# The gated memory mix: how x^T reaches the feed-forward part

## The chip, the cores and the metric

The kernel runs on one core of one Trainium2 chip. The metric is the device time of one execution in microseconds (us). A core has five engines that the text names: TensorE (PE in the profile, with its weight loads as PEld), VectorE (DVE), ScalarE (ACT), GpSimd (POOL) and SyncE (SP), which issues transfers. Each engine works through its own instructions in order and waits on semaphores for the others. Sixteen DMA engines serve the queues of SP, POOL and ACT together.

## What is computed

One input x of 2048 rows by 1024 columns (bf16) goes through two parts, and a gate per row mixes them.

```
g = sigmoid((x * gate_w).sum(-1, keepdims=True))
a = A(x)      # 64 segments of 32 rows, one after the other; 8 memory rows go from each to the next;
              # 32 heads of 128: q, k, v, softmax with a mask, output projection
b = (gelu(x @ w_gate) * (x @ w_up)) @ w_down      # the feed-forward part, inner width 3584
out = g * a + (1 - g) * b
```

## The kernel before

The whole program is one list of operations. `op(engine, make, r=..., w=..., dsem=...)` appends one; the keys in `r` and `w` name what it reads and writes, and the semaphore waits follow from them. The order of the list is the order on each engine: nothing reorders it afterwards. An operation with `dsem` is a DMA, issued by the engine named.

The feed-forward part runs first, in four blocks of 512 rows. A block has a gate/up phase and a down phase. In the gate/up phase 28 steps j (`emit_H`) each make 16 matmuls of 128x512 (L466): eight for the gate, eight for up, with 128 columns of weights as the stationary operand and the block's x^T as the moving one. The results lie in two PSUM banks. A step uses one of two bank pairs, so step j + 2 waits until step j's results are read. ScalarE squares the gate result (L472), VectorE forms the polynomial (L474), ScalarE takes the tanh (L477), and VectorE makes two products (L478 and L481), the second of which writes H and frees the bank. Down (`down_mm`, L511) multiplies H by the down weights in two halves of two row tiles; it uses the other four banks first.

The weights come by SP's queue. `next_slab` (L296) loads slabs of 512 columns, 1 MB each, into four chunks of a large SBUF tile named arena: two slabs after every fourth step, each waiting for TensorE to be done with the chunk that it overwrites. Block 0 also loads the down weights (`load_WD`, L440); blocks 1 and 2 copy weights to a scratch in DRAM for the later part (`copy_wide`, L675). The first two slabs come in halves (L294, L295), the second halves waiting for the last of the first four row tiles and for the first half of slab 0.

The moving operand is x^T: 128 partitions (columns of x within a group of 128), eight groups, 512 rows. x comes as sixteen row tiles t of 128 rows by 1024 columns, `load_rows` (L273): the first four on SP's queue at the very start, the others on POOL's queue into the same four buffers. `emit_xT(t)` makes eight TensorE transposes of 128x128 into a PSUM bank (L346) and one eviction from it into arena, on VectorE (L355), or on ScalarE for tiles 1 and 3 (L353). Between the first four tiles `spin` (L409) makes matmuls of the identity with itself whose result nobody reads: 2, 6, 2 and 8 of them. For tiles 4 to 15 the transposes stand at step j = 12, 16, 20 and 24 of the gate/up phase of the block ahead of the one that needs them.

Two more users of a row tile: `emit_cp(t, half)` copies its transposed rows out of the PSUM bank on ScalarE (L364, L365) in the order that the attention part wants, into xseg, and after the second half POOL issues the transfer of xseg to the scratch xT_scr in DRAM (L369). `emit_gate` multiplies the plain rows by gate_w and sums them on VectorE (L374, L379). The copies stand one and two steps behind the transposes (for the first four tiles: at j = 3t and 3t + 1).

The attention part follows: 64 segments in a written order (PLAN), which stream weights from the scratch through a ring of buffers. It starts after the last down phase.

Of the kernel before, what the change touches and what calls it, by code (L numbers as in the profile page):

```python
# [7 lines left out]
ACTF = mybir.ActivationFunctionType  # L8
# [18 lines left out]
class _Sched:  # L27
# [10 lines left out]
    def op(self, eng, mk, r=(), w=(), dsem=None):  # L38
        o = _Op(eng, mk, dsem)
        deps = []  # L40
        if eng == "pool" and dsem is None:
            w = [*w, ("pool",)]
        for k in r:
            deps += self.w.get(k, ())
            if k[0] == "P":
                deps += [x for x in self.r.get(k, ()) if x.eng != eng]
        for k in w:
            deps += self.w.get(k, ())
            deps += self.r.get(k, ())
        for k in r:  # L50
            self.r.setdefault(k, []).append(o)
        for k in w:
            self.w[k] = [o]
            self.r[k] = []
        seen = set()
        for d in deps:
            if d is o or id(d) in seen:
                continue
            seen.add(id(d))
            if d.eng == eng and d.dsem is None and (eng == "pe" or eng == "sp"):  # L60
                continue
            o.deps.append(d)
            d.sig = True
        self.ops.append(o)
        return o
# [63 lines left out]
def bass_gated_mix__memory_aug_recurrent_mem_tr__geglu_ffn__prompt_kernel(  # L129
# [15 lines left out]
    xf = A_x.flatten_outer_dims()  # L145
# [8 lines left out]
    KC = D // 128  # L154
# [13 lines left out]
    with ExitStack() as es:  # L168
# [23 lines left out]
        def SB(shape, dt, name):  # L192
            return es.enter_context(nc.sbuf_tensor(name, list(shape), dt))
# [20 lines left out]
        ident = SB([128, 128], BF16, "ident")  # L214
# [11 lines left out]
        PBV = [p[:, :].bitcast(BF16) for p in PB]  # L226

        def P(i):
            return ("P", i)

        g = _Sched()
        op = g.op
# [3 lines left out]
        A_X = (4, 5)  # L236
# [8 lines left out]
        def chunk(c):  # L245
            return arena[:, c * (CH // 2):min((c + 1) * (CH // 2), 21 * (CH // 2) + 2048)]

        def A(c):
            return ("A", c)
# [5 lines left out]
           r=[("ident",)], w=[("ident",)])  # L255
        xrow = [chunk(A_M[0])[:, i * 1024:(i + 1) * 1024] for i in range(4)]
        gwb = chunk(A_M[1])[:, 0:1024]
        gpr = chunk(A_M[1])[:, 1024:2048]
        xseg = chunk(A_M[1])[:, 2048:2048 + (GR + 1) * KC * SEG].rearrange("p (s kc c) -> p s kc c", s=GR + 1, kc=KC)
# [7 lines left out]
        misc_rows = A(A_M[0])  # L267
        misc_gate = A(A_M[1])
# [3 lines left out]
        def load_rows(t):  # L272
            op("sp" if t < 4 else "pool", lambda e: e.dma_start(xrow[t % 4], xf[t * 128:(t + 1) * 128, :]),  # L273
               r=[A(A_M[0])], w=[("xrow", t % 4)], dsem=f"xrow{t if t < 4 else t % 4 + 4}")

        for t in range(4):
            load_rows(t)

        def mk_gw(e):
            with nc.allow_non_contiguous_dma(reason="one row to all partitions"):  # L280
# [6 lines left out]
        def load_slab(i):  # L287
            b, jj, k = slabs[i]
            W = B_w_gate if k == "g" else B_w_up
            c = A_W[i % 4]  # L290
            dst = chunk(c).rearrange("p (kc c) -> p kc c", kc=KC)
            src = W[:, jj * 512:(jj + 1) * 512].rearrange("(kc p) c -> p kc c", p=128)
            if i < 2:
                op("sp", lambda e: e.dma_start(dst[:, :, 0:256], src[:, :, 0:256]), r=first[i], w=[("W", i)], dsem=f"rp{4 + i}")  # L294
                return lambda: op("sp", lambda e: e.dma_start(dst[:, :, 256:512], src[:, :, 256:512]), r=[("xrow", 3)] if i == 0 else [("W", 0)], w=[A(c)], dsem=f"a{c}")  # L295
            op("sp", lambda e: e.dma_start(dst, src), r=first[i] if i < 4 else [], w=[A(c)], dsem=f"a{c}")  # L296

        n_slab = [0]
# [1 line left out]
        def next_slab():  # L300
            if n_slab[0] < len(slabs):
                n_slab[0] += 1
                return load_slab(n_slab[0] - 1)

        for rest in [next_slab() for _ in range(2)]:
            rest()
        for _ in range(2):
            next_slab()

# [13 lines left out]
        for side in range(2):  # L323
            op("pool", lambda e, side=side: e.memset(bm[64 * side:64 * side + L, side:side + 1], 1.0),
               r=[("bm",)], w=[("bm",)])
# [10 lines left out]

        def emit_xT(t, eng="dve"):
            b, tt = t // 4, t % 4  # L340
            bank = t % 4 + (0 if b == 2 else 4)

            def mk(e):
                ins = None
                for kc in range(KC):
                    ins = e.transpose(PBV[bank][:, kc * 128:(kc + 1) * 128], xrow[t % 4][:, kc * 128:(kc + 1) * 128],  # L346
                                      ident[:, :])
                return ins
            op("pe", mk, r=[("xrow", t % 4), ("ident",), misc_rows], w=[P(bank)])
            dst = chunk(A_X[b % 2]).rearrange("p (kc r) -> p kc r", kc=KC)[:, :, tt * 128:(tt + 1) * 128]  # L350
            src = PBV[bank].rearrange("p (kc r) -> p kc r", kc=KC)
            if eng == "act":
                op("act", lambda e: e.activation(dst, src, ACTF.Copy), r=[P(bank), A(A_X[b % 2])], w=[("xT", t)])  # L353
            else:
                op("dve", lambda e: e.tensor_copy(dst, src), r=[P(bank), A(A_X[b % 2])], w=[("xT", t)])  # L355

        def emit_cp(t, half):
            bank = t % 4 + (0 if t // 4 == 2 else 4)
            pv = PBV[bank].rearrange("p (kc s c) -> p s kc c", kc=KC, s=4)

            def cp(e):
                ins = None
                for q in (2 * half, 2 * half + 1):
                    ins = e.activation(xseg[:, q, :, 0:NR], pv[:, q, :, EXT:SEG], ACTF.Copy)  # L364
                    ins = e.activation(xseg[:, GR, :, q * EXT:(q + 1) * EXT], pv[:, q, :, 0:EXT], ACTF.Copy)  # L365
                return ins
            op("act", cp, r=[P(bank), misc_gate, ("xseg0",)], w=[("xseg", half)])
            if half:
                op("pool", lambda e: e.dma_start(xT_scr[t, :, :], xseg.rearrange("p s kc c -> p (s kc c)")),  # L369
                   r=[("xseg", 0), ("xseg", 1), misc_gate], w=[("xTscr", t)], dsem="xseg")  # L370
# [34 lines left out]
        def spin(n):  # L405
            def mk(e):
                ins = None
                for _ in range(n):
                    ins = e.matmul(PB[3][:, 0:128], lhsT=ident[:, :], rhs=ident[:, :], start=True, stop=True)  # L409
                return ins  # L410
            op("pe", mk, r=[("ident",)], w=[P(3)])

        for t in range(4):
            emit_xT(t, ("dve", "act")[t % 2])
            spin((2, 6, 2, 8)[t])

        def emit_m0():
            def mk(e):
# [285 lines left out]
        for b in range(4):  # L704
            mine, other = (b % 2) * 4, 4 - (b % 2) * 4
            for j in range(NJ):
# [3 lines left out]
                if b == 0 and j < 12 and j % 3 < 2:  # L710
                    emit_cp(j // 3, j % 3)
# [7 lines left out]
                if b < 3 and j >= 12:  # L719
                    t = (b + 1) * 4 + (j - 12) // 4  # L720
                    if j % 4 == 0:
                        emit_xT(t)
                    elif j % 4 == 1:
                        emit_cp(t, 0)
                    elif j % 4 == 2:
                        emit_gate(t, 0)
                        emit_cp(t, 1)
                    else:
                        emit_gate(t, 1)
# [241 lines left out]
        for s in range(NSEG):  # L971
# [393 lines left out]
            if s == 0:  # L1365
                emit_P("q", 0, (0,))
                def zero(e):
# [4 lines left out]
                   w=[P(B_S), ("gp",)])  # L1372
# [10 lines left out]
                   w=[("bo", x) for x in range(4)])  # L1383
# [178 lines left out]
```

## Time and profile before

| | us |
|---|---|
| runs shown (three): median | 2209.19 |
| lowest and highest | 2204.6 and 2210.04 |
| the profiled execution | 2207.77 |
| its span, first to last instruction | 2205.9 |
| TensorE busy in it | 2104.6 |

Times in the profile count from the first instruction of the span. A row of the timeline begins with its start and its length in us, then the engine, the line of the kernel, the operation, and what it writes and reads; square brackets name how long the engine stood idle before it and who released it. SPq is SP issuing a transfer: the length is that of issuing, not of moving. A row of the DMA view ends with the size of one transfer and the median time from issue to landing of those issued in the stretch asked for. A row of busy time by stretch has, behind the stretch and its length, the busy time of PE, PEld, DVE, ACT and POOL with the number of instructions, the granted TensorE clock, the mean busy share of the sixteen DMA engines, and GB/s. A row of the DMA queues has packets, MB and their share of the sixteen engines' time. The granted TensorE clock of this execution is 0.994 of full speed in the mean.

### The profile page before, as it was taken

Reading aid. Unit: us, or ns where it says so; the run is one execution under the profiler, and the core shown is the slowest. Engines: PE = TensorE matmul, PEld = TensorE weight load, DVE = VectorE, ACT = ScalarE, POOL = GpSimd, SP = SyncE. Lnnn points to the kernel's source line nnn. Section 1 sums busy time; section 2 is a strip of 40 time slices with the busy share of each in tenths; the row PEclk is TensorE's granted clock in tenths of the full one; section 3 lists DMA queues with packets and bytes.
Section 4 is the critical chain, followed back from the end, with each engine's and each line's share of the span. In section 5 each row is a group of like instructions: output and inputs, shape, how many; then the busy total and the mean of one; then the engine's idle time right before and its main releaser. Section 6 shows DMA issues by size and latency. Waiting matters only on the chain.

```text
span 2205.9 us, 78545 instructions
## 1 busy us (share of the span) xinstructions
PE 2104.6 (95%) x35368; PEld 1107.8 (50%) x35424; DVE 1154.8 (52%) x2680; ACT 935.6 (42%) x1960; POOL 461.6 (21%) x814
## 2 busy tenths in 40 slices
PE   9999999999998999999999999999999999999987
PEld 4444444444454555555454545555455555555544
DVE  5716536345054555555555555555555555555554
ACT  4403324133044444544454445444444444444443
POOL 1020020140122222222122222222122222222221
PEclk9999999999999999999999999999999999999999
DMA  8726625346888999999999999999999999999997
GB/s 271 276 70 220 215 58 194 122 148 202 302 302 301 325 326 328 326 338 328 330 317 327 325 319 329 323 324 320 315 323 328 332 330 329 337 333 323 324 325 245
DMA packets 247377, 629.21 MB, mean 285 GB/s; under 512 B 37393, under 2 KB 106081, under 8 KB 246273
## 3 DMA queue, kind: packets, MB, share of 16 engines
q1 hardware_dynamic: 215732, 573.14, 74.5%
q0 software_dynamic: 30112, 50.48, 7.4%
q8 instruction: 278, 4.55, 0.8%
q10 hardware_dynamic: 1196, 0.56, 0.1%
q14 instruction: 59, 0.48, 0.1%
HBM read 596.71 MB, written 34.59 MB: 286 GB/s over the span
## 4 chain that ended last, share of the span: by engine, by line
PE 77%; DMA 15%; DVE 4%; ACT 2%; issue 2%; POOL 0%; SPq 0%; DVEq 0%; POOLq 0%; ACTq 0%
PE pba L1087 13%; PE pbb L1087 12%; DMA ring<-w_scr 11%; PE pbc L897 6%; PE pbb L1279 4%; DMA hT<-xT_scr 3%; PE pba L1279 3%; PE pbc L1258 3%; PE pba L466 2%; PE pbh L466 2%; PE pbg L466 2%; PE pbf L466 2%; PE pbe L466 2%; PE pbb L466 2%; PE pbd L466 2%; PE pbc L466 2%
## 5 line engine op out<-in xcount | busy, mean ns | idle before, releaser
L1087 PE MATMUL pba<-arena,hT 128*32 128x512 bf16 x4416 | 357.1, 383 | 5.1 <-DVE bo L1358 4.4
L1087 PE MATMUL pbb<-arena,hT 128*32 128x512 bf16 x4416 | 355.6, 383 | 1.3 <-issue 1.3
L897 PE MATMUL pbc<-arena,xe 128*32 128x512 bf16 x2208 | 190.0, 381 | 3.4 <-ACT rowsx L996 2.0
L803 POOL DMA_DIRECT2D vt<-v_scr x252 | 140.7, 561 | 146.8 <-PE pba L1087 94.3
L1087 PEld LDWEIGHTS pba<-arena,hT 128*32 128x32 bf16 x4416 | 109.2, 97 | 112.1 <-ACT rows L1074 11.0
L1087 PEld LDWEIGHTS pbb<-arena,hT 128*32 128x32 bf16 x4416 | 113.4, 97 | 99.2 <-DVE hT L1355 6.2
L1087 PE MATMUL pba<-ring,hT 128*32 128x512 bf16 x1286 | 127.2, 384 | 18.5 <-DMA ring<-w_scr 16.7
L1184 ACT ACTIVATE pbd<-pbd 104x320 f32<-104x320 f32 x128 | 53.0, 414 | 215.3 <-DVE pbd L1182 215.3
L1087 PE MATMUL pbb<-ring,hT 128*32 128x512 bf16 x1280 | 126.4, 384 | 7.8 <-DMA ring<-w_scr 7.2
L920 ACT ACTIVATE rows<-pba 128x512 bf16<-128x512 f32 (+1 forms) x130 | 67.1, 516 | 150.2 <-PE pba L1087 126.0
L1194 DVE TENSOR_TENSOR pn<-pbd,rr 104x512 bf16<-104x512 f32 (+1 forms) x256 | 125.7, 491 | 9.3 <-DVE rr L1189 0.6
L920 ACT ACTIVATE rows<-pbb 128x512 bf16<-128x512 f32 x127 | 66.0, 520 | 149.5 <-PE pbb L1087 119.5
L1026 POOL DMA_DIRECT2D qk_scr<-rowsx x60 | 47.5, 792 | 365.2 <-DVE pbd L1178 171.5
L1178 DVE SCALAR_TENSOR_TENSOR pbd<-pbd,mask 104x320 f32<-104x320 f32 x128 | 63.5, 496 | 102.0 <-PE pbd L1171 102.0
L1279 PE MATMUL pbb<-arena,oT 128*32 128x256 bf16 (+1 forms) x2304 | 115.8, 268 | 0.0
L1279 PE MATMUL pba<-arena,oT 128*32 128x256 bf16 (+1 forms) x2320 | 112.7, 269 | 0.1
L477 ACT ACTIVATE arena<-arena 128x512 f32<-128x512 f32 x112 | 70.5, 629 | 97.6 <-DVE arena L474 97.6
L821 POOL DMA_DIRECT2D bo<-b_scr x63 | 35.6, 565 | 341.8 <-PE pba L1087 235.9
L920 ACT ACTIVATE oT<-pbe 128x256 bf16<-128x256 f32 x192 | 73.6, 384 | 48.7 <-PE pbe L1231 47.4
L920 ACT ACTIVATE qk<-pbe 128x512 bf16<-128x512 bf16 x127 | 75.5, 594 | 36.4 <-PE pbe L1133 35.1
L1187 DVE TENSOR_REDUCE mx<-pbd 104x8 f32<-104x320 f32 x128 | 62.9, 491 | 53.5 <-ACT pbd L1184 53.5
L1133 PEld LDWEIGHTS pbe<-ident,rows 128*32 128x32 bf16 (+1 forms) x1560 | 46.0, 96 | 77.6 <-ACT rows L920 50.4
(308 smaller groups left out, 4519.5 us busy)
## 6 DMA issues: line engine op xcount, KB each, us to landing
ring<-w_scr SPq DMA_DIRECT2D x896, 512.0 KB, 5.5
arena<-in_B_w_gate_dram SPq DMA_DIRECT2D x27, 1024.0 KB, 5.4
arena<-in_B_w_up_dram SPq DMA_DIRECT2D x27, 1024.0 KB, 8.3
pn<-qk_scr POOLq DMA_DIRECT2D x63, 128.0 KB, 5.3
qk_scr<-rowsx POOLq DMA_DIRECT2D x60, 128.0 KB, 5.0
arena<-in_B_w_down_dram SPq DMA_DIRECT2D x7, 1024.0 KB, 11.4
arena<-in_A_Wk_dram SPq DMA_DIRECT2D x6, 1024.0 KB, 6.9
arena<-in_A_Wv_dram SPq DMA_DIRECT2D x6, 1024.0 KB, 10.1
```

Of the source, the lines that this page charges most:

```text
L466: ins = e.matmul(PB[bank][:, :], lhsT=wv[:, kc, col:col + 128], rhs=xb[:, kc, :], start=(kc == 0), stop=(kc == KC - 1))
L477: op("act", lambda e: e.activation(tp[q], tp[q], ACTF.Tanh, scale=C_GELU), r=[("tp", q)] + mr, w=[("tp", q)])
L803: op("pool", lambda e, side=side: e.dma_start(vt[p0 + side * EXT:p0 + (side + 1) * EXT, :, :], v_scr[s // GR, h, side::2, s % GR, :, :].re ...
L897: ins = e.matmul(PB[B_X][32 * gq:32 * gq + 32, :], lhsT=xe[:, us[-1], :], rhs=us[gq // 2][0][gq % 2], start=(n == 0), stop=(n == KC - 1), ...
L920: op("act", lambda e: e.activation(dst, src, ACTF.Copy), r=r, w=w)
L1087: ins = e.matmul(PB[bank][32 * gq:32 * gq + 32, :], lhsT=hT[:, kc, :], rhs=us[gq // 2][0][gq % 2], start=(x == 0), stop=(x == KC - 1), ski ...
L1178: op("dve", lambda e: e.scalar_tensor_tensor(out=sv, in0=sv, scalar=scale, in1=mask[0:104, None, :].to_broadcast([104, 8, L]), op0=ALU.mul ...
L1184: op("act", lambda e: e.activation(sv, sv, ACTF.Exp), w=[P(B_S)])
L1187: op("dve", lambda e: e.tensor_reduce(mxv, sv, AX.X, ALU.add), r=[P(B_S)], w=[("mx",)])
L1194: op("dve", lambda e, c0=c0, k0=k0, n=n: e.tensor_tensor(out=pn[0:104, :, c0:c0 + 2 * n].rearrange("p i (two c) -> p i two c", two=2), in0 ...
L1258: ins = e.matmul(PB[B_X][b:b + 32, :], lhsT=oe[:, o * 8 + k, :], rhs=u[c], start=(n == 0), stop=(n == H - 2), skip_group_check=True)
L1279: ins = e.matmul(PB[B_O][32 * q:32 * q + 32, c0:c1], lhsT=oT[:, o % 2, k, :], rhs=u[q // 2][:, (q % 2) * 256 + c0:(q % 2) * 256 + c1], sta ...
```

## The change

The sixteen tiles of x^T are no longer made on TensorE. Each is one transposing DMA from x in DRAM straight into arena, on SP's queue. The first four stand at the head of that queue, where the four plain row loads stood; the plain loads, still needed for the gate, follow behind the four half slabs. The others stay at the same place in the list (j = 12, 16, 20, 24), now as SP operations, and name no chunk that they would have to wait for. The second half of slab 0 waits for the transposed tile 3 where it waited for the plain one. The copies into xseg read arena, where they read PSUM, and so wait for the transposing DMA to land. The spins become one run of 48, behind which the first gate/up matmul stands.

```diff
+        def emit_xT(t):
+            dst = chunk(A_X[t // 4 % 2]).rearrange("p (kc r) -> p kc r", kc=KC)[:, :, t % 4 * 128:(t % 4 + 1) * 128]
+            op("sp", lambda e: e.dma_start_transpose(dst, xf[t * 128:(t + 1) * 128, :]),
+               w=[("xT", t)] + ([("xT", t - 8)] if t >= 8 else []), dsem="xt%d" % (t % 4))
+
         for t in range(4):
-            load_rows(t)
+            emit_xT(t)
...
-                return lambda: op("sp", lambda e: e.dma_start(dst[:, :, 256:512], src[:, :, 256:512]), r=[("xrow", 3)] if i == 0 else [("W", 0)], w=[A(c)], dsem=f"a{c}")
+                return lambda: op("sp", lambda e: e.dma_start(dst[:, :, 256:512], src[:, :, 256:512]), r=[("xT", 3)] if i == 0 else [("W", 0)], w=[A(c)], dsem=f"a{c}")
...
         for rest in [next_slab() for _ in range(2)]:
             rest()
+        for t in range(4):
+            load_rows(t)
         for _ in range(2):
             next_slab()
...
-        def emit_xT(t, eng="dve"):
-            b, tt = t // 4, t % 4
-            bank = t % 4 + (0 if b == 2 else 4)
...
-            op("pe", mk, r=[("xrow", t % 4), ("ident",), misc_rows], w=[P(bank)])
...
-                op("dve", lambda e: e.tensor_copy(dst, src), r=[P(bank), A(A_X[b % 2])], w=[("xT", t)])
-
         def emit_cp(t, half):
-            bank = t % 4 + (0 if t // 4 == 2 else 4)
-            pv = PBV[bank].rearrange("p (kc s c) -> p s kc c", kc=KC, s=4)
+            pv = chunk(A_X[t // 4 % 2]).rearrange("p (kc t s c) -> p t s kc c", kc=KC, t=4, s=4)[:, t % 4]
...
-            op("act", cp, r=[P(bank), misc_gate, ("xseg0",)], w=[("xseg", half)])
+            op("act", cp, r=[("xT", t), A(A_X[t // 4 % 2]), misc_gate, ("xseg0",)], w=[("xseg", half)])
...
-        for t in range(4):
-            emit_xT(t, ("dve", "act")[t % 2])
-            spin((2, 6, 2, 8)[t])
+        spin(48)
```

More of the change, by code (lines that the diff above doesn't have):

```diff
@@ L334, in bass_gated_mix__memory_aug_recurrent_mem_tr__geglu_ffn__prompt_kernel @@
         op("pool", lambda e: e.dma_start(m0, mem0[:, :]), r=[A(A_W[3])], w=[("oe", x) for x in range(NO)], dsem="m0")
-        def emit_xT(t, eng="dve"):
-            b, tt = t // 4, t % 4
-            bank = t % 4 + (0 if b == 2 else 4)
[L343 to L348, printed above, removed]
-            op("pe", mk, r=[("xrow", t % 4), ("ident",), misc_rows], w=[P(bank)])
[L350 to L354, printed above, removed]
-                op("dve", lambda e: e.tensor_copy(dst, src), r=[P(bank), A(A_X[b % 2])], w=[("xT", t)])
         def emit_cp(t, half):
-            bank = t % 4 + (0 if t // 4 == 2 else 4)
-            pv = PBV[bank].rearrange("p (kc s c) -> p s kc c", kc=KC, s=4)
+            pv = chunk(A_X[t // 4 % 2]).rearrange("p (kc t s c) -> p t s kc c", kc=KC, t=4, s=4)[:, t % 4]
             def cp(e):
```

## The prediction

> **What bounds the kernel now.** Page first, for the share of each engine and the chain of work that ended last.
>
> ```profile
> PE 2104.6 (95%) x35368; PEld 1107.8 (50%) x35424; DVE 1154.8 (52%) x2680; ACT 935.6 (42%) x1960; POOL 461.6 (21%) x814
> ...
> PE 77%; DMA 15%; DVE 4%; ACT 2%; issue 2%; POOL 0%; SPq 0%; DVEq 0%; POOLq 0%; ACTq 0%
> ```
>
> TensorE bounds the whole. The change touches the feed-forward part alone, so the second view is busy time by stretch: the first block's gate/up phase, its down phase, and block 1.
>
> ```profile
> 9.80:106.60 96.80, 95.99 (x467) 44.44 (x476) 68.22 (x100) 43.53 (x120) 9.93 (x18) 1.00 0.84 283
> 109.00:157.50 48.50, 48.24 (x222) 21.95 (x225) 4.25 (x7) 2.03 (x4) 6.35 (x12) 1.00 0.24 77
> 157.50:300.00 142.50, 141.81 (x673) 65.56 (x685) 69.88 (x102) 42.43 (x93) 15.62 (x28) 1.00 0.53 176
> ```
>
> TensorE (first number after the length) has no slack: whatever leaves its queue is gained, whatever makes it wait is lost. The DMA share (second last) is 0.84 in the first gate/up phase and 0.53 in block 1 as a whole: the new transfers go where DMA is busiest. The third view is the chain in order of time, here its start and one later transpose group.
>
> ```profile
> 3.70 1.03 PE pbe L346 x8
> ...
> 8.40 1.03 ACT arena L353
> ...
> 9.78 1.67 PE pba L466 x7
> ...
> 55.30 0.45 PE pbe L346 x8
> ```
>
> The first gate/up matmul (L466) starts at 9.78, after four transpose groups and the last eviction. A later group of eight transposes takes 0.45 us on the chain.
>
> **What is removed.** Four groups ahead of 9.78 (counted in the start below) and twelve later ones, 12 x 0.45 = 5.4 us of TensorE time; one of them stands where VectorE is late in block 0, so I count 5.3. Fourteen evictions leave VectorE and two leave ScalarE; save the last of the start (8.40), all lie beside TensorE: nothing. The copies to xseg (L364, L365) read SBUF now; ScalarE's 128x512 takes 0.63 us from SBUF (L477, the group below) and 0.60 from PSUM (L472, in a row further down), so a copy changes by some hundredths either way: nothing, under TensorE's cover.
>
> ```profile
> L477 ACT ACTIVATE arena<-arena 128x512 f32<-128x512 f32 x112 | 70.5, 629 | 97.6 <-DVE arena L474 97.6
> ```
>
> **What one transposing DMA costs (call it T, us of the sixteen DMA engines for 256 KB).** No row shows one. The nearest rows are queue 1 in two stretches with runs of 512 bytes (8 to 12 us) and longer ones (12 to 20 us).
>
> ```profile
> q1 hardware_dynamic: 2226, 1.12, 109.8%
> ...
> q1 hardware_dynamic: 2424, 2.27, 89.4%
> ```
>
> 64 us of engine time for 2226 packets of 503 bytes is 28.7 ns each; 0.894 x 128 us for 2424 of 936 bytes is 47.2 ns. That is 7.2 ns plus 0.043 ns a byte. A plain tile at 47.2 ns for 936 bytes would be 262144/936/16 x 47.2 ns = 0.8 us: the lower end. A transposed tile writes each source row across partitions; if it goes in 32-byte pieces, 8192/16 x 8.6 ns = 4.4 us: the upper end. I take the geometric middle, 1.9 us, because 256-byte reads alone (64 x 18.1 ns) already give 1.2 and the scattered write comes on top. The Trainium skill, "DMA: Bandwidth & Descriptors", Latency and other measured facts, gives a DMA transpose 261 GB/s with a non-contiguous middle dimension, an estimate of 1.0 us a tile; by that the sum below would be about zero. No run here shows it yet.
>
> **The start.** SP's queue and its waits:
>
> ```profile
> 0.75 1.84 SPq L273 DMA_DIRECT2D arena<-in_A_x_dram  x4
> ...
> 6.64 0.37 SPq L295 DMA_DIRECT2D arena<-in_B_w_gate_dram  x1
> 8.34 0.37 SPq L295 DMA_DIRECT2D arena<-in_B_w_up_dram  x1
> ```
> ```profile
> SPq L295 <- DMA arena<-in_A_x_dram: 2.6, 1, 2.6
> ...
> SPq L295 <- DMA arena<-in_B_w_gate_dram: 1.3, 1, 1.3
> ```
>
> SP sits on the last x tile until 6.64 and on the first half of slab 0 until 8.34; those are their landings. The four transposes take the place of the plain loads at the head of the queue, so both landings move by 4(T - 0.8). The matmul then waits for slab 0 instead of for an eviction: at T = 1.9 it starts at 8.34 + 4.4 + 0.2 = 12.9, which is 3.2 later than 9.78. Queued behind on SP are the slab halves and now the four plain x loads (1 MB, some 3 us), ahead of slabs 2 and 3, first needed four steps of 3.46 us (96.8 us over 28) after the start; the gate's VectorE work needs the rows later still: nothing. The clock:
>
> ```profile
> 8.16 0.85 PE L409 MATMUL pbd<-ident 128*128 128x128 bf16 x8
> ```
>
> The spins at the start cost 106 ns each against 56 later (0.45/8), a half-rate array from 3.70 to about 9. The 48 spins need 5.1 us at that rate and begin at the earliest when identity is built, so TensorE is idle for some us before 12.9. If the rate falls back, the same 5.3 us at half rate is 2.7 lost; bounds 0 and 2.7, I take 1.3. The Trainium skill, "TensorE: Matmul & The Clock Gate", Part 1, puts the fall at about 3.4 us of idling; nothing of before shows it. Start: +4.5.
>
> **The later twelve.** They stand in SP's queue behind weight transfers, and ScalarE, in order, now waits for their landing at L364, where it waited for TensorE. Behind that wait stand the next Square (L472), VectorE's three steps (L474, L478, L481), and TensorE, which needs L481 to free its banks two steps later. For t = 4 the transfer ahead is issued at 51.82 and lands 11.3 later (the DMA view of 51.80 to 51.87):
>
> ```profile
> 51.82 1.87 SPq L440 DMA_DIRECT2D arena<-in_B_w_down_dram  x2
> ```
> ```profile
> arena<-in_B_w_down_dram SPq DMA_DIRECT2D x1, 1024.0 KB, 11.3
> ```
> ```profile
> 60.67 0.31 ACT L364 ACTIVATE arena<-pbe 128x192 bf16<-128x192 bf16 x1
> ...
> 64.54 0.69 DVE L481 SCALAR_TENSOR_TENSOR arena<-arena,pba 128x512 bf16<-128x512 f32 x1
> ...
> 65.94 1.89 PE L466 MATMUL pba<-arena 128*128 128x512 bf16 x8
> ```
>
> It lands at 63.1 + T; ScalarE would copy at 60.67. Hidden is only 65.94 - 65.23 = 0.7. Stall: 63.1 - 60.67 - 0.7 + T = 1.7 + T. For t = 5 the queue is still full from t = 4, but TensorE has moved by that first stall: I put it at T - 1.4. The largest of block 1 is t = 10, behind a scratch copy (issued 228.03, landing 9.9 later):
>
> ```profile
> 228.03 0.73 SPq L675 DMA_DIRECT2D w_scr<-in_A_Wv_dram  x1
> ...
> w_scr<-in_A_Wv_dram SPq DMA_DIRECT2D x1, 512.0 KB, 9.9
> ...
> 235.13 0.31 ACT L364 ACTIVATE arena<-pbc 128x192 bf16<-128x192 bf16 x1
> ...
> 236.70 0.60 ACT L472 ACTIVATE arena<-pbe 128x512 f32<-128x512 f32 x1 [0.80 <-PE pbe L466]
> ...
> 239.50 0.69 DVE L481 SCALAR_TENSOR_TENSOR arena<-arena,pbe 128x512 bf16<-128x512 f32 x1
> ...
> 241.68 0.59 PE L466 MATMUL pbe<-arena 128*128 128x512 bf16 x2
> ```
>
> 237.9 - 235.13 = 2.8 late, less ScalarE's idle 0.8 and 241.68 - 240.19 = 1.5 of slack: 0.5 + T. t = 8 (issue 199.51, +8.4, copy 206.61) gives T - 1.0 and t = 9 (213.77, +9.2, copy 220.87) T - 0.2 in the same way:
>
> ```profile
> 199.51 0.59 SPq L675 DMA_DIRECT2D w_scr<-in_A_Wk_dram  x1
> ...
> 213.77 1.31 SPq L675 DMA_DIRECT2D w_scr<-in_A_Wv_dram  x2
> ...
> 206.61 0.31 ACT L364 ACTIVATE arena<-pba 128x192 bf16<-128x192 bf16 x1
> ...
> 220.87 0.31 ACT L364 ACTIVATE arena<-pbb 128x192 bf16<-128x192 bf16 x1
> ```
> ```profile
> w_scr<-in_A_Wk_dram SPq DMA_DIRECT2D x1, 512.0 KB, 8.4
> ...
> w_scr<-in_A_Wv_dram SPq DMA_DIRECT2D x1, 512.0 KB, 9.2
> ```
>
> Block 2's tiles stand right behind a slab with nothing between. For t = 13 that slab is issued at 360.18 and lands 8.1 later, against a copy at 367.70:
>
> ```profile
> 360.18 0.37 SPq L296 DMA_DIRECT2D arena<-in_B_w_up_dram  x1
> ...
> arena<-in_B_w_up_dram SPq DMA_DIRECT2D x1, 1024.0 KB, 8.1
> ...
> 367.70 0.31 ACT L364 ACTIVATE arena<-pbf 128x192 bf16<-128x192 bf16 x1
> ```
>
> 0.6 late, 2.3 hidden as at t = 10: T - 1.7. I price t = 6, 12 and 14, likewise behind a slab, with it. The last tile of each block (7, 11, 15) costs nothing: after its copy come two gate/up steps whose banks are free, then 24 us of down-projection on the other four banks; without that cover it would cost like its neighbours. At T = 1.9: 3.6 + 0.5 + 0.9 + 1.7 + 2.4 + 4 x 0.2 = 9.9. The same late copies delay the xT_scr writes on POOL's queue and the x loads behind them; these are read at the recurrence hundreds of us later: nothing. The recurrence itself is unchanged.
>
> **Sum.** 4.5 - 5.3 + 9.9 = +9.1. The profiled execution took 2207.77 us (span 2205.9), 1.4 under the median 2209.19; 2207.77 + 9.1 = 2216.9, against the median **2218**, +0.4%. At T = 0.8: start -1.2 (slab 0 at 8.34), -5.3, stalls 2.5 + 0.6 + 1.3 = 4.4: -2.1. At T = 4.4: +13.2 + 2.7 - 5.3 + (6.1 + 3.0 + 3.4 + 4.2 + 4.9 + 10.8) = +43.
>
> **Rivals.** (1) The transposed tile is as cheap as a plain one: T below about 1.1, where the sum crosses zero. For it speaks that both read 256 KB of DRAM on sixteen engines; against it the short pieces. Time 2207; with every wait hidden as well, -6.5, 2202.7. (2) The scattered write dominates, T of 3 to 4.4: +25 to +43, 2234 to 2252. For it speaks the fixed 7.2 ns a packet. (3) The tile's eight 128-wide blocks go one after the other, each a small transfer:
>
> ```profile
> b_scr<-ring POOLq DMA_DIRECT2D x2, 16.0 KB, 1.9
> ```
>
> at 1.9 us to land (0 to 120 us), T = 15: start +56, nine stalls some 130, about 2390. Against it: the sixteen-engine queue shows no such serial transfer. The Trainium skill, "VectorE: DVE Perf Modes", The three transpose paths, lists 1309 ns for a 128x128 DMA transpose against 390 on TensorE, a rule against this change; eight of those are an estimate of 10.5 us a tile, some 2330.
>
> **Chances.** Forecast (T 1.4 to 3, 2212 to 2234) 0.47; rival 1 0.30; rival 2 0.15; rival 3 0.08. Under 0.3% (6.6 us) a measurement tells no difference, and T = 1.7 is where the sum passes it: faster 0.05 (the far end of rival 1), same 0.35 (the rest of it and the forecast's low end), slower 0.60. Range 2204 to 2255, which leaves out rival 3 and the ends of 1 and 2.
>
> **What would show it.** On the page L346 and L355 are gone. SP's first wait on x should end at 6.64 + 4.4 = 11, the first L466 start near 13, its first matmuls perhaps at half rate. ScalarE's L364 should wait on a DMA into arena, longest at t = 4 and t = 10, and TensorE on L481 two steps later by 2 to 4 us. A DMA row of the transposes gives T at once: 1.0 at the head of the queue makes rival 1, 10 rival 3. The forecast is wrong if a tile does not keep its place in the queue, so that waits vanish or grow without T, or if TensorE's banks have more slack than these rows give.

## The result, and the profile after

The changed kernel takes 2219.66 us in the median of 20 runs (2208.09 to 2231.89), the kernel before 2206.95 in 20 runs beside it (2201.54 to 2210.98). The ratio is 1.006, 95% interval 1.0046 to 1.0074: 12.7 us slower, where 9 were forecast.

The profiled execution of the changed kernel happens to be the fastest of its twenty. So its stages are read, not its total. Engine shares and chain on its page:

```profile
PE 2101.1 (95%) x35326; PEld 1099.8 (50%) x35326; DVE 1145.3 (52%) x2666; ACT 935.3 (42%) x1958; POOL 460.9 (21%) x814
...
PE 71%; DMA 16%; DVE 7%; ACT 3%; issue 2%; SPq 0%; POOL 0%; DVEq 0%; ACTq 0%
```

Against before, VectorE's share of the chain is 7% where it was 4%: TensorE now waits for VectorE's steps. Busy time by stretch, first of the kernel before (first gate/up phase, the rest of the feed-forward part, the attention part), then of the changed one:

```profile
0.00:108.90 108.90, 103.61 (x528) 50.72 (x539) 71.87 (x105) 47.64 (x124) 13.25 (x39) 1.00 0.82 274
108.90:596.00 487.10, 484.68 (x2260) 222.76 (x2304) 203.72 (x298) 123.08 (x249) 59.32 (x110) 1.00 0.51 167
596.00:2205.90 1609.90, 1516.28 (x32584) 834.31 (x32582) 879.21 (x2278) 764.84 (x1588) 388.98 (x666) 0.99 0.93 322
```
```profile
0.00:119.40 119.40, 106.11 (x503) 48.63 (x504) 64.62 (x94) 44.38 (x114) 12.96 (x38) 0.96 0.90 267
119.40:608.90 489.50, 485.23 (x2242) 218.38 (x2240) 201.10 (x295) 126.47 (x258) 59.48 (x110) 1.00 0.55 170
608.90:2206.30 1597.40, 1509.75 (x32584) 832.76 (x32582) 879.54 (x2278) 764.44 (x1588) 388.44 (x666) 1.00 0.93 324
```

The feed-forward part ends 12.9 us later (608.9 against 596.0), 10.5 of it in the first gate/up phase. The attention part, which the change does not touch, is 12.5 us shorter in this one execution; in the fourteen profiles of this case it takes between 1596 and 1610 us, so that difference is scatter. The 12.9 us agree with the 12.7 between the medians.

Where it goes is read from the starts of the steps in TensorE's timeline, the gate matmuls of step j of a block, before and after:

| block, step | before | after | later by |
|---|---|---|---|
| 0, 0 | 9.78 | 11.20 | 1.42 |
| 0, 1 | 13.02 | 16.69 | 3.67 |
| 0, 6 | 30.29 | 36.71 | 6.42 |
| 0, 8 | 37.19 | 44.08 | 6.89 |
| 0, 15 | 62.49 | 69.27 | 6.78 |
| 0, 16 | 65.94 | 76.12 | 10.18 |
| 0, 17 | 69.84 | 81.26 | 11.42 |
| 1, 0 | 157.46 | 168.00 | 10.54 |
| 2, 0 | 304.28 | 315.88 | 11.60 |
| 3, 0 | 451.11 | 463.97 | 12.86 |

Three things add up: the start (3.7), a jump at steps 6 to 8 (3.2), and after that 6.0 net, in which some 5.2 us of saved transposes are already counted, so 11 us of stalls. (The row of before at 9.78 has seven of the eight matmuls; if the one that is not recorded is the first, step 0 is 1.6 later and not 1.4.) The rows of TensorE's timeline at the start, the jump and the two longest later stalls:

```profile
11.20 3.59 PE L452 MATMUL pba<-arena 128*128 128x512 bf16 x8 [5.13 <-DMA arena<-in_B_w_gate_dram]
...
36.71 1.90 PE L452 MATMUL pba<-arena 128*128 128x512 bf16 x8 [2.59 <-DVE arena L467]
...
76.12 2.96 PE L452 MATMUL pba<-arena 128*128 128x512 bf16 x8 [3.23 <-DVE arena L467]
...
401.52 1.89 PE L452 MATMUL pba<-arena 128*128 128x512 bf16 x8 [2.19 <-DVE arena L467]
```

L452 is the old L466, L467 VectorE's last step of H (old L481), L352 the copy to xseg (old L364). SP's queue, which in the rows of before had the plain loads at its head:

```profile
0.75 5.41 SPq L278 DMA_TRANSPOSE arena<-in_A_x_dram  x4
6.21 0.58 SPq L299 DMA_DIRECT2D arena<-in_B_w_gate_dram  x1
...
8.62 0.81 SPq L300 DMA_DIRECT2D arena<-in_B_w_gate_dram  x1
11.17 0.37 SPq L300 DMA_DIRECT2D arena<-in_B_w_up_dram  x1
...
59.41 7.70 SPq L278 DMA_TRANSPOSE arena<-in_A_x_dram  x1
```

Issuing four transposes takes SP 5.41 us (four plain loads took 1.84), and one issued into a full queue 7.70. So the first half of slab 0 is issued at 6.21, where it was at 2.63, and is down at 11.17, where it was at 8.34. ScalarE's waits in the gate/up phases, summed, and the two at the jump and at tile 4:

```profile
ACT arena L352 <- DMA arena<-in_A_x_dram: 29.2, 12, 4.9
...
ACT arena L352 <- DMA xT_scr<-arena: 5.3, 2, 4.9
```
```profile
32.37 0.36 ACT L352 ACTIVATE arena<-arena 128x192 bf16<-128x192 bf16 x1 [4.86 <-DMA xT_scr<-arena]
...
71.69 0.36 ACT L352 ACTIVATE arena<-arena 128x192 bf16<-128x192 bf16 x1 [4.58 <-DMA arena<-in_A_x_dram]
```

All twelve later tiles are late for ScalarE. The wait at 32.37 is another one: the buffer xseg is not free, since its write to xT_scr has not landed. That wait was not forecast.

### The profile page after: what moved, and what is told of

The parts are those of the page before. It is cut to its first block, busy times and chain, and to the rows that moved or that the text cites. A ratio compares the mean times of both kernels' runs of the same rounds, so it can differ in the third digit from the quotient of the medians.

```text
span 2206.3 us, 78419 instructions
## 1 busy us (share of the span) xinstructions
PE 2101.1 (95%) x35326; PEld 1099.8 (50%) x35326; DVE 1145.3 (52%) x2666; ACT 935.3 (42%) x1958; POOL 460.9 (21%) x814
## 4 chain that ended last, share of the span: by engine, by line
PE 71%; DMA 16%; DVE 7%; ACT 3%; issue 2%; SPq 0%; POOL 0%; DVEq 0%; ACTq 0%
PE pba L1073 12%; PE pbb L1073 12%; DMA ring<-w_scr 11%; PE pbc L883 6%; PE pbb L1265 4%; PE pba L1265 3%; PE pbc L1244 3%; DMA arena<-in_A_x_dram 2%; PE pbe L1190 2%; PE pbe L1119 2%; PE pbd L1157 2%; PE pbe L1217 2%; DMA hT<-xT_scr 2%; PE pbe L452 2%; PE pbh L452 2%; PE pbg L452 2%
## 5 line engine op out<-in xcount | busy, mean ns | idle before, releaser
L1073 PE MATMUL pba<-ring,hT 128*32 128x512 bf16 x1286 | 128.4, 383 | 12.7 <-DMA ring<-w_scr 11.8
```

The lines of the kernel that those rows point to most:

```text
L1073: ins = e.matmul(PB[bank][32 * gq:32 * gq + 32, :], lhsT=hT[:, kc, :], rhs=us[gq // 2][0][gq % 2], start=(x == 0), stop=(x == KC - 1), ski ...
```

## The experiments

"Later by" means the start of the last step of block 3 against the kernel before, in the profiles; it tells a few us apart where the whole time scatters by more. Ratios are whole times against the kernel before on the same chip. bare_price, pool_free and spin_long were run once, so only their profiles are read.

### One part alone: the start, and the later tiles

start_only gives tiles 4 to 15 back to TensorE, with eviction and copies as before (code shortened here and below).

```diff
-        def emit_xT(t):
+        def emit_xT(t, eng="dve"):
+            if t >= 4:
+                return emit_xT_pe(t, eng)
```

> Only tiles 0 to 3 come by transposing DMAs; tiles 4 to 15 are transposed on TensorE and evicted as before. Theory (the loss is the sum of two separate parts, a late start and late copies): the down part of block 3 begins about 6.9 us later than in the kernel before, 3.7 of it at the first gate/up steps and some 3 at step 6, where ScalarE waits for xT_scr; no later wait at the copies; time about 2214. Rival (the start is made up for later, and the twelve later tiles cost everything): under 1 us later, 2207.

later_only does the reverse: `if t < 4`, with the loads and spins of the start as before.

> Only tiles 4 to 15 come by transposing DMAs; the first four and the start are as before. Theory: the first gate/up matmul is back at 9.8 us, ScalarE waits some 29 us in total at the copies for the transposed tiles, and the feed-forward part ends about 6 us later than before; time about 2213. Rival (the start costs everything): 5 us earlier than before, 2202.

start_only: later by 7.9 us, ratio 1.0043 (1.0019 to 1.0067). later_only: 4.5 us, ratio 1.0027 (1.0002 to 1.0053). Together 12.4, against 12.9 for the whole change: the two parts add up, and the start weighs more than the later tiles. That they agree so closely is in part chance, since the jump at steps 6 and 7 is 5.4 us in start_only's profile and 3.2 in the changed kernel's. In start_only the loss is complete at step 7 (8.6 us); nothing after it stalls. In later_only the first matmul is back at 9.65 us, and ScalarE's waits for tiles are as in the whole change:

```profile
ACT arena L374 <- DMA arena<-in_A_x_dram: 28.7, 11, 5.8
```

### Is it the transposing, or the place in the queue?

plain_rows puts a plain DMA of the same bytes, in the same 256-byte pieces, where each transposing DMA stands; arena then holds x untransposed.

```diff
-            op("sp", lambda e: e.dma_start_transpose(dst, xf[t * 128:(t + 1) * 128, :]),
+            op("sp", lambda e: e.dma_start(dst, xf[t * 128:(t + 1) * 128, :].rearrange("r (kc c) -> r kc c", kc=KC)),
```

> Every transposing DMA becomes a plain one of the same 256 KB to the same place, at the same point of SP's queue; so arena holds x untransposed and the products are of other numbers. Theory (the place behind the weights makes two thirds of the lateness, the transfer itself one third): ScalarE's waits for the tiles shrink from 29 us to 15 to 18, the start is 1 to 4 us earlier, and the feed-forward part ends 2 to 5 us later than before. Rival (the transposing itself, its slow transfer and the 4 to 8 us that SP is busy issuing one, makes nearly all): waits under 5 us, and the part ends 5 us earlier than before, 2202.

Neither held. The waits for tiles are not smaller at all, ratio 1.0066 (1.0045 to 1.0088):

```profile
ACT arena L352 <- DMA arena<-in_A_x_dram: 28.9, 11, 5.5
...
ACT arena L352 <- DMA xT_scr<-arena: 9.3, 2, 8.2
```

A plain tile at the same place is as late as a transposed one, though SP issues it in 0.6 to 1.6 us and not in 3.7 to 7.7. So for the later tiles the place behind the weights makes the lateness, and neither the transposing nor SP's long issue does. The start is quicker (step 1 later by 1.8, not 3.7), and there SP's issuing has a part in it: the first slab goes out 1.8 us sooner than in the changed kernel, and the first matmul starts 1.3 sooner.

```profile
0.75 3.67 SPq L278 DMA_DIRECT2D arena<-in_A_x_dram  x4
4.45 0.88 SPq L299 DMA_DIRECT2D arena<-in_B_w_gate_dram  x1
```

The jump at steps 6 and 7, 8.7 us here, is larger than in the changed kernel and hides that; it is taken up below.

bare_price measures a tile by itself: the kernel before, with eight transposing DMAs added in block 0's down phase and eight plain ones in block 1's, all into a chunk that nobody reads at that time.

```diff
+            if b < 2:
+                for i in range(8):
+                    dst = chunk(A_X[b]).rearrange("p (kc r) -> p kc r", kc=KC)[:, :, i % 4 * 128:(i % 4 + 1) * 128]
+                    # b == 0: dma_start_transpose(dst, x tile i); b == 1: dma_start of the same bytes; both wait for the last H
```

> The kernel before with two things added where DMA is nearly idle and nothing waits for them: in block 0's down phase eight transposing DMAs of 256 KB, in block 1's eight plain DMAs of the same bytes to the same places, each in two runs of four. Theory from the plain-rows run (a transposed tile costs hardly more of the DMA engines than a plain one): four back to back take 4 to 6 us transposed and 3.5 to 5 plain. Rival (my estimate of 1.9 us a tile against 0.8): 7.6 us and more against 3.2.

The DMA view of a stretch in which only the transposed tiles move, and of one with only the plain ones:

```profile
DMA packets 4576, 1.14 MB, mean 190 GB/s; under 512 B 4576, under 2 KB 4576, under 8 KB 4576
```
```profile
DMA packets 4280, 1.08 MB, mean 216 GB/s; under 512 B 4280, under 2 KB 4280, under 8 KB 4280
```

That is 262144 bytes in 1.38 us transposed and 1.21 us plain, or 5.5 and 4.9 for four: the theory of this run. But the two are not limited by the same thing. SP issues the transposing DMAs 1.35 us apart (at 123.47, 124.82, 126.17 and 127.52) without waiting for anything, and the DMA engines' busy share, here in tenths over 40 slices of each stretch, falls between them; in the plain stretch they are busy throughout:

```profile
DMA  0999678799999433799999523799999945897999
```
```profile
DMA  9999999999999999999999999999999999999999
```

So 1.38 us is SP's pace, and an upper bound on what a transposed tile costs the DMA engines. From 120.0 to 121.1 us, with issued tiles still queued, they moved at 286 GB/s, from which I estimate 0.92 us a tile. That the transposing itself costs the DMA engines anything is not shown; a plain tile in 256-byte pieces costs more than my 0.8 us.

### Earlier tiles, later copies

If the place is the cause, there are two cures: issue the tiles earlier, or read them later. early_four issues tiles 4 to 15 at steps 8, 12, 16 and 20.

```diff
+                if b < 3 and 12 - 4 <= j < 28 - 4 and (j + 4) % 4 == 0:
+                    emit_xT((b + 1) * 4 + (j + 4 - 12) // 4)
                 if b < 3 and j >= 12:
                     t = (b + 1) * 4 + (j - 12) // 4
-                    if j % 4 == 0:
-                        emit_xT(t)
-                    elif j % 4 == 1:
+                    if j % 4 == 1:
```

> Tiles 4 to 15 are issued four steps (some 14 us) earlier in SP's queue, at steps 8, 12, 16 and 20; the copies stay where they are. Theory (late copies): ScalarE's waits for the tiles fall from 29 us to under 5, TensorE's waits on L467 after step 12 vanish, and the feed-forward part ends 1 to 3 us later than before instead of 12.9; time about 2209. Rival (SP, busy issuing a transpose, holds up the slabs behind it): the same waits move to TensorE waiting for slabs, and the time stays at 2219.

Not one wait of ScalarE for a tile is left, and from step 8 to the end the kernel gains 5.4 us (from 11.7 late to 6.3), as much as the saved transposes. Late copies were the later tiles' whole loss. The total is higher than expected (ratio 1.0043, 1.0017 to 1.0068) because the jump at steps 6 and 7 is 8.6 us in this profile.

later_early joins the early tiles with the start of the kernel before.

> The start as in the kernel before (tiles 0 to 3 on TensorE), tiles 4 to 15 by transposing DMAs issued four steps earlier than in the changed kernel. Theory (with the place in the queue mended only the gain is left): the feed-forward part ends 5 to 6 us earlier than before, 12 times 0.45 us; time about 0.25% under the kernel before. Rival (a transposing DMA costs something wherever it stands): no earlier than before.

Later by -0.2 us, not -5 to -6; ratio 0.9996 (0.9978 to 1.0014). From block 1 on it gains all of its 0.45 us a tile, but block 0 loses 5.2 us up to step 13, 1.6 of it in the jump at steps 6 to 8 and 3.6 at steps 12 and 13. Busy time by stretch, 45 to 65 us, of this kernel and of the kernel before:

```profile
45.00:65.00 20.00, 17.09 (x71) 7.13 (x71) 13.66 (x20) 6.99 (x19) 2.69 (x5) 0.91 1.16 297
```
```profile
45.00:65.00 20.00, 19.59 (x96) 9.03 (x97) 15.17 (x24) 9.91 (x29) 2.69 (x5) 1.00 0.89 315
```

The DMA share is 1.16 (the view counts overlapping packets) against 0.89, although fewer bytes move (297 GB/s against 315), and ScalarE waits 3.7 us for xT_scr at 50.96: what the tile no longer loses, the write behind it does. That the fuller queues make this wait is argued from these rows and tested only by the next kernel. eight_early leaves tiles 4 to 7 on TensorE, too (`if t < 8`, the others early).

> Tiles 0 to 7 on TensorE as in the kernel before; only tiles 8 to 15 (issued in blocks 1 and 2) by transposing DMAs, four steps earlier than in the changed kernel. Theory (block 0 has no DMA time to spare, blocks 1 and 2 have): the feed-forward part ends 3.6 us earlier than before, 8 times 0.45 us; ratio about 0.9984. Rival (the DMAs cost something in any block): less than 1.5 us earlier.

Earlier by 4.5 us, ratio 0.9986 (0.9963 to 1.0009): the gain is in the trace, and the whole time cannot tell it from none. Of the 4.5, 0.96 is there at the end of block 0, where this kernel is the kernel before; so much do two profiles of the same instructions differ, and the change's own gain is the 3.6 of eight groups.

copies_late moves the reader: start as before, tiles 4 to 15 at the place of the changed kernel, copies four steps later.

```diff
                     elif j % 4 == 1:
-                        emit_cp(t, 0)
+                        if j > 16:
+                            emit_cp(t - 1, 0)
...
+                emit_cp(b * 4 + 7, 0)          # ahead of the down phase
+                emit_cp(b * 4 + 7, 1)
```

> The start as in the kernel before, tiles 4 to 15 by transposing DMAs at the place of the changed kernel, and the copies to xseg four steps later (those of a block's last tile ahead of its down phase). Theory (only ScalarE's in-order wait for the tile costs; the DMA's place does not): no wait for a tile, and the feed-forward part ends 4 to 5.4 us earlier than before. Rival (the extra transfers in block 0 hold up other transfers by themselves): a loss of 2 us or more stays in block 0 and the part ends less than 3 us earlier.

Ratio 0.997 (0.9949 to 0.9991): faster than both kernels. In its profile no wait for a tile is left and the part ends 1.9 us earlier; it would be 6.1 but for a jump of 4.1 us at steps 6 and 7, which this execution has although its start is that of before.

### The jump at step 6: POOL's queue

The first write to xT_scr stands on POOL behind the loads of gate_w and mem0, which wait for slabs 2 and 3. pool_free lets both wait for slab 0.

```diff
-        op("pool", mk_gw, r=[A(A_M[1]), A(A_W[2])], w=[("gwb",)], dsem="gwb")
+        op("pool", mk_gw, r=[A(A_M[1]), A(A_W[0])], w=[("gwb",)], dsem="gwb")
-        op("pool", lambda e: e.dma_start(m0, mem0[:, :]), r=[A(A_W[3])], w=[("oe", x) for x in range(NO)], dsem="m0")
+        op("pool", lambda e: e.dma_start(m0, mem0[:, :]), r=[A(A_W[0])], w=[("oe", x) for x in range(NO)], dsem="m0")
```

> As the changed kernel, but on POOL's queue the loads of gate_w and mem0 wait for slab 0 instead of slabs 2 and 3, so that the first xT_scr write behind them is issued earlier. Theory (POOL's queue, held by slabs that land later now, makes the stall at step 6): ScalarE's wait for xT_scr falls from 5.3 us to under 1.5, the jump at step 6 is gone, and the feed-forward part ends 9 to 10.5 us later than before instead of 12.9. Rival (the transfers at the start are slow in themselves): the jump stays.

The jump is gone (step 8 later by 3.5, not 6.9), and the part ends 8.4 us later, not 12.9. POOL issues the write before SP's next pair of slabs, where in the changed kernel it comes behind the first of them. The two rows, of pool_free and of the changed kernel:

```profile
21.49 0.57 POOL L357 DMA_DIRECT2D xT_scr<-arena  x1 [5.45 <-ACT arena L353]
```
```profile
26.16 0.54 POOL L341 DMA_DIRECT2D oe<-in_A_mem_dram  x1 [2.85 <-DMA arena<-in_B_w_up_dram]
26.70 0.57 POOL L357 DMA_DIRECT2D xT_scr<-arena  x1
```

The order explains the size in all fourteen profiles of this case: with the write ahead of that pair (before, pool_free and four more) ScalarE waits for it 0 to 0.6 us; with it between the two slabs 3.4 to 5.8 (the changed kernel 4.9, start_only 5.8, copies_late 4.7, bare_price 4.6, later_early 3.4); with it behind both (early_four, plain_rows, spin_long) 7.7, 8.2 and 8.8. In the kernel before it goes out at 20.88 and the pair from 21.91: one microsecond of luck, which the late start uses up. bare_price, whose instructions are those of the kernel before up to 108 us, has no such luck: its write goes out at 22.22, behind the slab of 21.40, and its step 7 comes 2.3 us later than its step 5 would have it. So the kernel before can lose this too, and some of what the profiles differ by at steps 6 and 7 is chance.

### The clock at the start

spin_long has 130 spins in place of 48.

> As the changed kernel, but with 130 spins instead of 48, which end at some 10.5 us, close to the first gate/up matmul. Theory (TensorE's rate falls in the 5 us of idling between the spins and the first matmul): the first step takes 3.5 us instead of 5.5, and step 1 starts 1.4 us later than before instead of 3.7. Rival (the rate of the first step has to do with the matmuls themselves): step 1 stays 3.7 us late.

```profile
1.54 9.64 PE L397 MATMUL pbd<-ident 128*128 128x128 bf16 x130 [1.54 <-POOL ident L253]
11.85 1.67 PE L452 MATMUL pba<-arena 128*128 128x512 bf16 x7 [0.67 <-DMA arena<-in_B_w_gate_dram]
14.94 1.90 PE L452 MATMUL pbb<-arena 128*128 128x512 bf16 x8 [1.42 <-DMA arena<-in_B_w_up_dram]
```

The rate is kept (the first matmuls of step 0 in 1.7 us and not 3.6), as the theory had it, but step 1 is just as late, 3.66 us: the quick matmuls wait for the up half of the weights, which lands at 14.9. That is this execution's own: in the changed kernel the same half, issued at 6.84, lands 6.1 later, at 12.96, when quick matmuls would just have come to it. So there the slow clock does cost: its step 0 takes 5.5 us and not 3.45, 2.0 lost. all_three below has the same 130 spins and an up half that lands at 12.7, and its step 1 is 1.9 late:

```profile
11.67 1.67 PE L452 MATMUL pba<-arena 128*128 128x512 bf16 x7
13.18 1.89 PE L452 MATMUL pbb<-arena 128*128 128x512 bf16 x8
14.91 1.89 PE L452 MATMUL pbc<-arena 128*128 128x512 bf16 x8
```

Why the half came two microseconds later in spin_long stays open. The part ends 18.4 us late in that profile, with a jump of 8.2.

### All together

all_three puts early tiles, the POOL edit and 130 spins onto the changed kernel.

> The changed kernel with three edits: tiles 4 to 15 issued four steps earlier, POOL's gate_w and mem0 loads waiting for slab 0, 130 spins. Theory (late copies, POOL's queue and the clock are the whole loss beside a start 1.4 us later): the feed-forward part ends 3 to 5 us earlier than before; time 0.1 to 0.25% under the kernel before. Rival (something else is lost in the first block): later than before.

Later by 0.5 us, ratio 1.0018 (1.0000 to 1.0036). Step 1 is 1.9 late, the jump is gone, but block 0 loses 2.0 us at step 12, where later_early lost 2.4. The rival was right that something else is lost in the first block.

late_and_pool is copies_late with the POOL edit.

> The copies-late kernel with one more edit: POOL's gate_w and mem0 loads wait for slab 0 instead of slabs 2 and 3. Theory (the jump of 4 us at steps 6 and 7 of the copies-late profile is again xT_scr behind POOL's slab waits): the jump is gone, the feed-forward part ends 5 to 6.5 us earlier than before, and the ratio is 0.996 to 0.998. Rival (the jump comes from the DMA engines being full): it stays in the profile and the ratio is no better than 0.997.

The jump is gone, and the part ends 6.0 us earlier than before: 5.4 for the twelve groups, and 0.6 that is no more than the first block of eight_early differed by with nothing changed. Ratio 0.9971 (0.9951 to 0.9992), 2197.82 us against 2204.85: better than both kernels, and not to be told from copies_late.

## Why the prediction was right, and where it was not

The sum, 9.1 us, came near 12.7 with two of its terms off in opposite directions and one missing. That it came so near is in part luck: with T = 1.38 its own formula gives 3.6, and with 0.9 about nothing, the time of rival 1. A price too high stood in for losses that it did not have.

- **The price of a tile, T.** 1.9 us was too high. bare_price gives 1.38 back to back, which is SP's pace, and the first four tiles of the changed kernel are issued at the same pace. Behind the weights it is less still: tile 4 lands 0.8 us behind the load ahead of it (issued at 58.78 and 59.41, in the two rows below), and nine of the twelve later tiles 0.8 to 1.0.

```profile
arena<-in_B_w_down_dram SPq DMA_DIRECT2D x1, 1024.0 KB, 12.1
...
arena<-in_A_x_dram SPq DMA_TRANSPOSE x1, 12.3
```

The failing step was the geometric middle between a plain tile and one written in 32-byte pieces: no run shows the scattered write coming on top, and the 256-byte read price alone, 1.2, is what plain tiles in such pieces took (1.21). The fit behind it was rough, too: it took the engines' time of the first row as 64 us, where 109.8% is 70.3, or 31.6 ns a packet and not 28.7. The Trainium skill's estimate of 1.0 us ("DMA: Bandwidth & Descriptors", Latency and other measured facts) is below the 1.38 us of SP's pace and above the 0.92 us of queued tiles, so as a price on the DMA engines the trace agrees with it. Rival 3, eight blocks one after the other, is out.
- **The start.** 4.5 forecast, 3.7 measured at step 1. That the matmul would wait for slab 0 was right, with 11.2 for the forecast 12.9; but what delays the slab is at least in part that SP is busy issuing four transposes (5.41 us, where plain loads took 1.84), a cost that the prediction did not have, and not their price on the DMA engines. The clock's share was forecast at 1.3, with bounds 0 and 2.7; in the changed kernel it is 2.0. So a landing put too late and a clock put too cheap made the start come out near. That the fall is real, and when it occurs, is in the granted clock (the third number from the end of each row) of the first matmuls, of the idle gap and the matmuls at step 16, and around the stall at 401.52:

```profile
11.20:14.60 3.40, 3.40 (x9) 1.20 (x10) 0.00 (x0) 0.00 (x0) 0.00 (x0) 0.50 1.21 292
...
73.00:76.10 3.10, 0.00 (x0) 0.01 (x1) 2.19 (x4) 1.99 (x7) 0.00 (x0) 1.00 1.06 353
76.10:81.30 5.20, 5.18 (x17) 2.01 (x18) 4.18 (x6) 1.42 (x3) 1.08 (x2) 0.67 1.18 279
397.00:404.00 7.00, 4.81 (x23) 2.08 (x22) 3.92 (x6) 4.47 (x13) 0.54 (x1) 1.00 0.88 278
```

- **The missing term.** "The gate's VectorE work needs the rows later still: nothing" looked at the wrong user. The later slabs also hold POOL's loads, POOL's loads hold the first xT_scr write, and that write holds ScalarE's next copy: 3.2 us at steps 6 to 8. start_only has the stall without the later tiles, and in pool_free and late_and_pool it is gone. The prediction followed POOL's queue only for the tiles of later blocks.
- **The later tiles.** 9.9 forecast, 11 measured, and the mechanism step by step as described: landing behind the weights, ScalarE's in-order wait, VectorE, TensorE two steps on. Tile 4: ScalarE's wait 4.6 against 2.4 + T = 4.3, TensorE's 3.4 against 3.6, but not by T: the tile took less, and the load ahead of it more (12.1 us to land for 11.3). Not priced was that an idle gap of 3.2 us also drops the clock; that adds 1.2 us at step 17. Block 1 came out smaller, 2.8 against 5.0, as it should with T smaller. Block 2 came out larger, 3.0 against 0.6: "right behind a slab with nothing between" is false for tile 14, which has two loads of later weights ahead of it in SP's list, and it is that tile that costs 2.3 us. Tiles 7, 11 and 15 cost nothing, as said, though tile 7 is 4.9 us late for ScalarE.
- **T as the lever.** The forecast tied the loss to T; plain_rows shows that the tie is weak. Rival 1, a transposed tile as cheap as a plain one, is what the later tiles show (0.8 to 1.0 us behind the weights), and its conclusion (no loss) was wrong, because the place alone is enough to make a loss.
- **What was hidden stayed hidden.** No run shows a gain from the evictions off VectorE and ScalarE: what late_and_pool gains, 6.0, is the 5.4 of the transposes but for 0.6.

A question left open is why the attention part differs by up to 14 us between single executions of the same instructions; it made the profile of the changed kernel look like no change at all.

## What to carry to other kernels

Before a transfer takes the place of engine work, look at what stands ahead of it in its queue and at who reads the result first: here the same bytes were late by their place, plain or transposed, and moving a reader that had time of its own turned a loss of 0.3% (later_only) into a gain of 0.3% (copies_late). A transfer moved to the head of a queue delays everything behind it, and the delay travels through other queues that wait for those transfers; follow each of them to an engine before writing "nothing". And where one microsecond of order between two queues decides over a stall, that order is luck and is worth fixing by itself.

## What the runs showed of the hardware

- Transposing DMAs of 128 rows by 1024 bf16, issued back to back by SP, moved at 190 GB/s, and at 286 while issued ones were queued; plain ones in the same 256-byte pieces moved at 216 with the DMA engines busy throughout (bare_price).
- Issuing one costs SP 1.35 us at the start (5.41 for four) and 3.7 to 7.7 us behind weights; a plain DMA in the same pieces took 0.9 (3.67 for four) and 0.6 to 1.6 (plain_rows). Behind the weights the longer issue cost nothing here; at the head of the queue it held back the first slab.
- In the changed kernel TensorE's granted clock fell after an idle gap of 3.2 us (0.67 over the 5.2 us that follow) and stayed at 1.00 through gaps of 2.6 and 2.2. In other profiles it fell after shorter ones, 2.3 us in copies_late (0.50 from 33.17 to 36.58) and 2.7 in later_early, and not after 2.3 in all_three, so the length of a gap alone does not decide. The Trainium skill, "TensorE: Matmul & The Clock Gate", Part 1, names about 3.4 us of idling; these falls came after less. The first spins run at 106 ns each though the records give their clock as 1.00, so that row does not show the first slow phase.
